# How many of a kernel's first loads may be in flight, and whether q goes ahead of w_in

## The chip, the cores and the metric

The kernel runs on one core of one Trainium2 chip. The metric is the time of one execution on the device in microseconds (us), taken as the median of several runs. Besides the plain runs one execution is recorded by the hardware profiler; all views below come from that one.

## The reference

Attention over a memory of 32 slots per head, followed by a feed-forward layer with SiLU. There are 8 batches, 8 heads, 576 positions and a head width of 64.

```python
a = softmax(phi, axis=2)                       # over the positions
k_m = einsum('bhsm,bhsd->bhmd', a, k)          # 32 memory keys per head
v_m = einsum('bhsm,bhsd->bhmd', a, v)          # 32 memory values per head
attn = softmax(q @ k_m.T / 8, axis=-1)         # over the 32 slots
x = (attn @ v_m) -> (4608, 512)
out = silu(x @ w_in) @ w_out                   # 512 -> 2048 -> 512
```

The weights are shared by all batches; `w_in` and `w_out` come in as raw 64-bit words and are turned into the format that TensorE uses by integer steps on ScalarE and VectorE.

## The kernel before

The work goes batch by batch (`for b in range(B)`, L875), and within a batch over 16 chunks of 128 columns of the hidden layer (`fc`). For a chunk, TensorE computes the hidden layer (`ffn1`, L627, line L642), ScalarE takes SiLU of it (`silu`, L662), VectorE splits it into a high and a low part (`split`, L651), and TensorE multiplies both with `w_out` (`ffn2`, L676, line L681). The attention of batch b+1 is laid between the chunks of batch b by a table of slots (L713 to L757).

Batch 0 has nothing before it. Its attention is written out by hand in the first block (L769 to L857), and in that block the instructions of VectorE and ScalarE stay in the order in which they are written (`in_order(DVE, ACT)`), as do those of TensorE throughout and those of SyncE's queue in batch 0. So an instruction that waits holds up all that stands behind it on its engine. The steps of the block that matter here, in order:

1. `load_phi(0)` (L217) and `load_kv(0)` (L226) issue the first loads. Batch 0's `kv` comes in four tiles and a rest (`kv0` to `kv3`, `kr`), all on ScalarE's DMA queue.
2. The loop over `LOADS` (L773) issues what follows, all on SyncE's queue: `i0` and `i1` are the two halves of the first piece of `w_in` (512 KB each), `Q0` and `Q1` the two halves of batch 0's `q` (576 KB each), `o0` and `o1` the two halves of the first piece of `w_out`, and each `L` a whole piece of weights.
3. `phi_max`, `phi_sub`, `phi_exp`: softmax numerators of phi, in two halves. `e_mm` (L319): memory keys and values, one `kv` tile after the other (L327), then the rest (L335), then the scaling to `kvn` (L349, L351).
4. `w_conv(I0, 0, "pc")` (L792): ScalarE's two steps (L167, L169) on the first half of the first piece of `w_in`, the one that `i0` loads.
5. `f_tr`, `f_vt` (L474), `f_scores(0)` (L485, needs `Q0`), `f_copy(0)` (L503 on ScalarE, L504 on VectorE), `f_turn(0)` (L517), `f_scores(1)` (L485, needs `Q1`), `f_max`, `f_sub` and so on, to the first chunk of the feed-forward layer.

`keep_warm` puts dummy matmuls of the identity between these steps on TensorE.

Loads that carry `few=True` wait, on SyncE, until an earlier load has landed: `load` (L86) keeps a list of all loads in the order of the program and ties the new one to the fifth before it.

Of the kernel before, what the change touches and what calls it, by code (L numbers as in the profile page):

```python
# [39 lines left out]
PHW = FULLC * HM + P  # L40
KVC = 2 * NR * KVW
RAWB = 3
LOADS = "i0 Q0 Q1 i1 o0 o1 L L L"
HOMES = {("o", 1): 8, ("i", 2): 12}
DEEP = 5


@with_exitstack
def attn_ffn_kernel(
# [34 lines left out]
    loads = []  # L84

    def load(dst, src, few=False, queue=None):  # L86
        i = (queue or nc.sync).dma_start(dst, src)
        if few:
            tc.add_manual_dep(
                i.ins,  # L90
                loads[-DEEP].ins.name,
                mybir.DependencyInfo(mybir.DependencyClass.Sync, mybir.DependencyReason.DATA),
                reason="few at a time",
            )
        loads.append(i)
# [25 lines left out]
    def w_load(w, part=None, few=False):  # L121


        kind, j = w
        if w not in raws:
            if w in HOMES:
                home = win[:, HOMES[w] : HOMES[w] + 4].rearrange("p k r f -> p (k r f)")
                raws[w] = home.bitcast(I64).rearrange("p (k f) -> p k f", k=2)
            else:
                raws[w] = sb.tile([P, 2, DMODEL], I64, tag="raw", name="raw", bufs=RAWB)  # L130
        if kind == "i":
            for k in range(2) if part is None else (part,):
                f = (2 * j + k) * P
                load(
                    raws[w][:, k].rearrange("p (r f) -> p r f", r=NR),
                    w_in[:, f : f + P].rearrange("(r p) f -> p r f", p=P),
                    few,
                )
        else:
            src = w_out[j * CW : (j + 1) * CW, :].rearrange("(r p) f -> p r f", p=P)  # L140
            load(w_part(raws[w], part), w_part(src, part), few)
# [75 lines left out]
    def load_phi(b):  # L217
        t = sb.tile([P, PHW], F32, tag="att", name=f"phi{b}")
        at[b]["e"] = t[:, : FULLC * HM].rearrange("p (g c f) -> p g c f", g=2, c=FULLC)
        at[b]["er"] = t[:, FULLC * HM :]  # L220
        at[b]["et"] = t
        w = FULLC * P
        for f in ((0, w), (2 * w, PHW), (w, 2 * w)) if b == 0 else ((0, PHW),):
            load(t[:, f[0] : f[1]], phi[b, :, f[0] : f[1]], queue=nc.scalar if f[0] == w else None)

    def load_kv(b):  # L226
        queue = nc.scalar if b == 0 else None
        ts = []
        for c in range(FULLC):
            t = sb.tile([P, 2, NR, KVW], F32, tag="kv", name=f"kv{b}_{c}", bufs=FULLC)  # L230
            load(t.rearrange("p g r f -> p (g r f)"), kv[b, :, c * KVC : (c + 1) * KVC], queue=queue)
            ts.append(t)
        t = sb.tile([P, NR, KVW], F32, tag="kr", name=f"kr{b}", bufs=1)
        load(t.rearrange("p r f -> p (r f)"), kv[b, :, FULLC * KVC :], queue=queue)
        at[b]["kv"], at[b]["kr"] = ts, t
# [533 lines left out]
    with in_order(DVE, ACT) as last:  # L769
        load_phi(0)  # L770
        nc.scalar.activation(tiny[:, :1], ident[:, :1], AF.Exp)
        load_kv(0)
        for c in LOADS.split():  # L773
            if c[0] == "Q":
# [181 lines left out]
```

## Time and profile before

| what | value |
|---|---|
| median of 3 runs | 703.94 us (703.69 to 704.26) |
| the profiled execution | 703.34 us |
| its span, first to last instruction | 701.6 us |
| granted TensorE clock, mean | 1.000 of full speed |
| busy share of TensorE, VectorE, ScalarE | 98%, 52%, 37% |
| chain that ended last: TensorE's share of it | 85% of the span |

The span is 1.7 us shorter than the profiled execution's time; the rest lies before the first and behind the last instruction. A busy TensorE includes the dummy matmuls. The share of busy time is an average over the whole program: the loads that the change touches are all issued in the first 15 us.

### The profile page before, as it was taken

How to read it: one execution, taken by the hardware profiler on the slowest of the kernel's cores; microseconds unless marked ns; L12 is line 12 of the kernel's file. 1: busy time of each engine (PE TensorE's matmuls, PEld its weight loads, DVE VectorE, ACT ScalarE, POOL GpSimd, SP SyncE). 2: the span in 40 equal slices, each digit the busy share in tenths (PEclk: the TensorE clock that was granted, in tenths of full speed). 3: DMA queues.
4: the chain of work that ended last, by engine and by line, in shares of the span. 5: the costliest groups of instructions: out<-in, count | busy, mean ns of one | idle time of the engine just before them, and what ended most of it. 6: DMA issues, size and time to landing. Idle time of an engine off the chain costs nothing.

```text
span 701.6 us, 11773 instructions
## 1 busy us (share of the span) xinstructions
PE 689.8 (98%) x4924; PEld 562.3 (80%) x4924; DVE 365.3 (52%) x665; ACT 259.1 (37%) x456; POOL 0.7 (0%) x6
## 2 busy tenths in 40 slices
PE   8999989999999999999999999999999999999997
PEld 3578768888888888888888888888888888888886
DVE  4898796425645256534636346542564525623322
ACT  3879674422414134421423314342241412431211
POOL 0000000000000000000000000000000000000000
PEclk9999999999999999999999999999999999999999
DMA  9995616122210221131110311112121000010002
GB/s 344 325 329 202 250 53 230 56 83 68 79 31 24 114 68 35 61 137 68 36 61 16 137 45 56 64 43 94 68 79 32 1 1 1 1 61 1 1 0 76
DMA packets 25445, 60.15 MB, mean 86 GB/s; under 512 B 2096, under 2 KB 10416, under 8 KB 25392
## 3 DMA queue, kind: packets, MB, share of 16 engines
q1 hardware_dynamic: 24448, 56.63, 22.8%
q10 hardware_dynamic: 944, 2.77, 1.0%
q8 instruction: 39, 0.64, 0.4%
q14 instruction: 14, 0.11, 0.0%
HBM read 49.95 MB, written 9.44 MB: 85 GB/s over the span
## 4 chain that ended last, share of the span: by engine, by line
PE 85%; DVE 1%; ACT 1%; issue 0%; ACTq 0%
PE acc L681 46%; PE h L642 26%; PE accleft L681 6%; PE bg L607 4%; PE h L327 2%; PE bg L372 1%; PE h L335 0%; PE h L357 0%; ACT L665 0%; DVE sc L420 0%; DVE wo_lo L177 0%; DVE raw L173 0%; PE h L372 0%; ACT wo_hi L175 0%; DVE sc L402 0%
## 5 line engine op out<-in xcount | busy, mean ns | idle before, releaser
L681 PE MATMUL acc<-wo_hi,gparts 128*128 128x512 f32 x1024 | 342.0, 395 | 1.0 <-DVE gparts L659 0.5
L681 PEld LDWEIGHTS acc<-wo_hi,gparts 128*128 128x128 f32 x1024 | 191.9, 188 | 54.2 <-issue 6.6
L642 PEld LDWEIGHTS h<-aparts,pparts 128*128 128x128 f32 x1524 | 213.9, 188 | 15.1 <-issue 2.5
L642 PE MATMUL h<-aparts,pparts 128*128 128x288 f32 x1524 | 223.1, 295 | 1.5 <-ACT gleft L667 1.2
L665 ACT ACTIVATE g<-h 128x512 f32<-128x512 f32 x127 | 76.1, 599 | 348.4 <-PE h L642 179.3
L681 PE MATMUL acc<-wo_lo,gparts 128*128 128x512 f32 x512 | 200.9, 392 | 0.6 <-DVE wo_lo L177 0.5
L657 DVE CAST gparts<-g 128x512 fp32r<-128x512 f32 x128 | 54.5, 426 | 261.0 <-ACT g L665 261.0
L681 PEld LDWEIGHTS acc<-wo_lo,gparts 128*128 128x128 f32 x512 | 96.1, 188 | 18.4 <-DVE wo_lo L177 1.9
L659 DVE TENSOR_TENSOR gparts<-g,gparts 128x512 fp32r<-128x512 f32 x128 | 88.2, 689 | 11.0 <-PE acc L681 0.5
L623 DVE TENSOR_TENSOR pparts<-bg,pparts 128x1024 fp32r<-128x1024 f32 (+1 forms) x36 | 39.7, 1102 | 5.4 <-ACT pparts L621 5.1
L681 PE MATMUL accleft<-wo_hi,gparts 128*128 128x512 f32 x128 | 40.6, 389 | 0.0
L621 ACT ACTIVATE pparts<-bg 128x1024 fp32r<-128x1024 f32 (+1 forms) x36 | 33.5, 931 | 14.3 <-PE bg L607 14.3
L607 PE MATMUL bg<-win,kvT 64*32 64x512 f32 (+1 forms) x576 | 35.8, 554 | 0.0
L681 PEld LDWEIGHTS accleft<-wo_hi,gparts 128*128 128x128 f32 x128 | 24.0, 188 | 4.9
L667 ACT ACTIVATE gleft<-h 128x64 f32<-128x64 f32 x127 | 27.8, 219 | 0.0
L688 ACT ACTIVATE o<-acc 128x512 f32<-128x512 f32 x32 | 19.2, 600 | 21.5 <-PE acc L681 10.6
L681 PE MATMUL accleft<-wo_lo,gparts 128*128 128x512 f32 x64 | 24.9, 389 | 0.0
L665 ACT ACT_TABLE_LOAD x14 | 18.0, 1283 | 14.1 <-issue 13.5
L657 DVE CAST gparts<-gleft 128x512 fp32r<-128x512 f32 x16 | 6.8, 427 | 20.7 <-PE accleft L681 12.2
L169 ACT ACTIVATE raw<-raw 128x1024 int32<-128x1024 uint32 (+1 forms) x16 | 16.9, 1053 | 0.0
L327 PEld LDWEIGHTS h<-kv,phi 128*32 128x32 f32 x384 | 10.2, 110 | 5.0 <-ACT gleft L667 5.0
L681 PEld LDWEIGHTS accleft<-wo_lo,gparts 128*128 128x128 f32 x64 | 12.0, 188 | 2.4
(139 smaller groups left out, 365.5 us busy)
## 6 DMA issues: line engine op xcount, KB each, us to landing
kv<-in_kv SPq DMA_DIRECT2D x28, 516.0 KB, 5.7
q<-in_q SPq DMA_DIRECT2D x16, 576.0 KB, 5.2
out<-o SPq DMA_DIRECT2D x32, 256.0 KB, 2.1
raw<-in_w_in SPq DMA_DIRECT2D x14, 512.0 KB, 6.4
raw<-in_w_out SPq DMA_DIRECT2D x6, 1024.0 KB, 5.3
phi<-in_phi SPq DMA_DIRECT2D x7, 576.0 KB, 3.7
kv<-in_kv ACTq DMA_DIRECT2D x4, 516.0 KB, 6.2
kr<-in_kv SPq DMA_DIRECT2D x7, 258.0 KB, 6.9
```

Of the source, the lines that this page charges most:

```text
L169: i = nc.scalar.activation(r, low, AF.Copy, scale=2.0**-29)
L327: nc.tensor.matmul(pt[p][M * r : M * (r + 1), :KVW], e[:, p, c, M * r : M * (r + 1)], kvt[c][:, p, r], start=c == 0, stop=False, skip_grou ...
L607: nc.tensor.matmul(bg[M * r : M * (r + 1), p, :w].rearrange("p (k f) -> p k f", f=P), kvT[D * p : D * (p + 1), 1, r], win[D * p : D * (p + ...
L621: nc.scalar.activation(hi[:, :, c], bg[:, :, :w], AF.Copy)
L623: nc.vector.tensor_tensor(lo[:, :, c], bg[:, :, :w], hi[:, :, c], op=ALU.subtract)
L642: nc.tensor.matmul(h[:, hf, :HALF], wt[:, p, fs], a[:, p, hf * HALF : (hf + 1) * HALF], start=n[hf] == 0, stop=n[hf] == 5, skip_group_chec ...
L657: nc.vector.tensor_copy(ghi, g32)
L659: nc.vector.tensor_tensor(glo, g32, ghi, op=ALU.subtract)
L665: nc.scalar.activation(g32.rearrange("p (h f) -> p h f", h=2), h[:, :, :w], AF.Silu)
L667: i = nc.scalar.activation(gleft[:, fc, o : o + LEFT].rearrange("p (h f) -> p h f", h=2), h[:, :, w:HALF], AF.Silu)
L681: nc.tensor.matmul(acc[key], gt[:, cs], wt[:, fc], start=fc == 0 and n == 0, stop=fc == NFC - 1 and n == 2)
L688: nc.scalar.activation(o, a, AF.Copy)
```

## The change

`LOADS` names `Q0` ahead of `i0`, so that each half of `q` stands in front of a half of `w_in`'s piece. And `load` ties a load to the third load before it rather than the fifth, as long as fewer than 11 loads are on the list.

```diff
-LOADS = "i0 Q0 Q1 i1 o0 o1 L L L"
+LOADS = "Q0 i0 Q1 i1 o0 o1 L L L"
 HOMES = {("o", 1): 8, ("i", 2): 12}
-DEEP = 5
+DEEP, FIRST_DEEP = 5, 3
...
             tc.add_manual_dep(
                 i.ins,
-                loads[-DEEP].ins.name,
+                loads[-(FIRST_DEEP if len(loads) < 11 else DEEP)].ins.name,
```

Eight loads stand on the list when the loop over `LOADS` begins: three of phi, then `kv0`, `kv1`, `kv2`, `kv3` and `kr`. So the new number holds for the loop's first three loads alone, which are now `Q0`, `i0` and `Q1`. What each load waits for:

| load | before | now |
|---|---|---|
| `i0` | `kv0` | `kv3` |
| `Q0` | `kv1` | `kv2` |
| `Q1` | `kv2` | `kr` |
| `i1` | `kv3` | `kv3` |
| `o0` | `kr` | `kr` |
| `o1` | `i0` | `Q0` |
| the two loads of the first `L` | `Q0`, `Q1` | `i0`, `Q1` |

On SyncE's queue, these are the first loads of the loop before. `raw<-in_w_in` is `i0`, later `i1`; `raw<-in_w_out` is `o0`; each `DMAHW` is a semaphore that a load raises when it lands, here those of `kv0` (3), `kv1` (4), `kv2` (5), `kv3` (7) and `kr` (1):

```order
L87 DMA phi_79<-in_phi 128x128
L87 DMA raw<-in_w_in 128x4x128 [waits DMAHW3_49]
L87 DMA q_0_96<-in_q 128x1152 [waits DMAHW4_49,DMAHW0_49]
L87 DMA q_1_98<-in_q 128x1152 [waits DMAHW5_49,DMAHW2_49]
L87 DMA raw<-in_w_in 128x4x128 [waits DMAHW7_49]
L87 DMA raw<-in_w_out 128x512 [waits DMAHW1_49]
```

And now, where `kv2` raises 5, `kv3` 6 and `kr` 7:

```order
L87 DMA phi_79<-in_phi 128x128
L87 DMA q_0_94<-in_q 128x1152 [waits DMAHW5_49,DMAHW0_49]
L87 DMA raw<-in_w_in 128x4x128 [waits DMAHW6_49,DMAHW1_49]
L87 DMA q_1_98<-in_q 128x1152 [waits DMAHW7_49,DMAHW2_49]
L87 DMA raw<-in_w_in 128x4x128 [waits DMAHW3_49]
L87 DMA raw<-in_w_out 128x512 [waits DMAHW4_49]
```

`i0` moved behind `Q0` and from `kv0`'s landing to that of `kv3`; `i1` and `o0` follow `Q1` without a wait of their own that is still open then. The waits on 0, 1 and 2 are for phi.

On ScalarE, in the same stretch, the order stays and the semaphores change hands:

```order
 L87 DMA kv_3_90<-in_kv 128x1032
-L87 DMA kr_92<-in_kv 128x516 [waits DMAHW1_49]
-L316 ACTIVATE phi_79<-phi_79 128x512 [waits DVE_49]
+L87 DMA kr_92<-in_kv 128x516
+L316 ACTIVATE phi_79<-phi_79 128x512 [waits DMAHW1_49,DVE_49]
 L317 ACTIVATE phi_79<-phi_79 64x128 [waits DMAHW2_49,DVE_49]
 L316 ACTIVATE phi_79<-phi_79 128x512 [waits DMAHW0_49,DVE_49]
 L317 ACTIVATE phi_79<-phi_79 64x128 [waits DVE_49]
 L349 ACTIVATE kvn<-first_152,rs 128x2x64 [waits DVE_49,PE_49]
-L167 ACTIVATE win<-raw 128x512 [waits DMAHW6_49]
+L167 ACTIVATE win<-raw 128x512 [waits DMAHW1_49]
```

The issue of `kr` no longer waits for a part of phi, whose semaphore it shared. `L167` still waits for `i0`, by another semaphore, and still stands ahead of `L474` and `L503` on ScalarE. TensorE's and VectorE's instructions keep their order.

## Rows read from the trace of the kernel before

**Rows 1.** The page, busy us (share of the span) x instructions of each engine

```profile
PE 689.8 (98%) x4924; PEld 562.3 (80%) x4924; DVE 365.3 (52%) x665; ACT 259.1 (37%) x456; POOL 0.7 (0%) x6
```

**Rows 2.** Stretches: us, busy us (x instructions) of PE, PEld, DVE, ACT, POOL, clock, DMA share, GB/s

```profile
17.00:31.00 14.00, 12.35 (x80) 7.47 (x80) 12.28 (x24) 11.44 (x22) 0.00 (x0) 1.00 1.06 366
31.00:60.00 29.00, 28.55 (x203) 22.19 (x202) 26.84 (x42) 23.75 (x33) 0.00 (x0) 1.00 0.81 289
```

**Rows 3.** Timeline of SyncE's DMA issues, 5 to 13 us: start us, us, what

```profile
5.82 0.38 SPq L87 DMA_DIRECT2D raw<-in_w_in  x1
7.62 0.34 SPq L87 DMA_DIRECT2D q<-in_q  x1
8.88 0.33 SPq L87 DMA_DIRECT2D q<-in_q  x1
10.27 0.38 SPq L87 DMA_DIRECT2D raw<-in_w_in  x1
11.39 1.22 SPq L87 DMA_DIRECT2D raw<-in_w_out  x2
```

**Rows 4.** DMA issues at 5.82 (i0) and 7.62 (Q0): KB, us to landing

```profile
raw<-in_w_in SPq DMA_DIRECT2D x1, 512.0 KB, 6.5
...
q<-in_q SPq DMA_DIRECT2D x1, 576.0 KB, 6.1
```

**Rows 5.** DMA queues, 5.8 to 9, then 9 to 11 us: packets, MB, share of 16 engines

```profile
q10 hardware_dynamic: 344, 1.23, 100.0%
...
q1 hardware_dynamic: 444, 0.47, 65.6%
q10 hardware_dynamic: 157, 0.31, 39.8%
```

**Rows 6.** DMA issues of w_in at 35.98, 61.84 and 62.26: KB, us to landing

```profile
raw<-in_w_in SPq DMA_DIRECT2D x1, 512.0 KB, 3.6
...
raw<-in_w_in SPq DMA_DIRECT2D x1, 512.0 KB, 3.9
...
raw<-in_w_in SPq DMA_DIRECT2D x1, 512.0 KB, 4.9
```

**Rows 7.** Timeline of ScalarE, 9.5 to 15 us: start us, us, what [idle before <-releaser]

```profile
9.57 0.63 ACT L316 ACTIVATE phi<-phi 128x512 f32<-128x512 f32 x1 [0.83 <-DVE phi L306]
...
12.64 0.37 ACT L349 ACTIVATE kvn<-first,rs 128x128 f32<-128x128 f32 x1 [2.11 <-DVE rs L345]
12.91 0.66 ACT L167 ACTIVATE win<-raw 128x512 f32<-128x512 f32 x1
13.47 0.67 ACT L169 ACTIVATE raw<-raw 128x512 int32<-128x512 uint32 x1
14.03 0.25 ACT L474 COPY kvT<-firstt 128x128 f32<-128x128 f32 x1
14.69 0.37 ACT L503 COPY sT<-firsts 128x256 f32<-128x256 f32 x1 [0.41 <-PE firsts L485]
```

**Rows 8.** Timeline of TensorE's matmuls, 9 to 16.5 us

```profile
9.18 0.87 PE L327 MATMUL first<-kv,phi 128*32 128x129 f32 x24
...
10.29 1.31 PE L327 MATMUL first<-kv,phi 128*32 128x129 f32 x40 [0.25 <-DMA kv<-in_kv]
11.53 0.45 PE L335 MATMUL first<-kr,phi 64*32 64x129 f32 x16
...
13.88 0.72 PE L485 MATMUL firsts<-q,kvT 64*32 64x288 f32 x16
14.54 0.60 PE L79 MATMUL spare<-ident 128*128 128x512 bf16 x2
15.12 0.66 PE L517 MATMUL firstu<-ident,sT 128*128 128x128 f32 x4
15.70 0.71 PE L485 MATMUL firsts<-q,kvT 64*32 64x288 f32 x16
```

**Rows 9.** Timeline of VectorE, 15 to 19 us

```profile
15.81 0.69 DVE L540 TENSOR_REDUCE fmx<-firstu 128x16 f32<-128x512 f32 x1
...
18.08 0.82 DVE L540 TENSOR_REDUCE fmx<-firstu 128x20 f32<-128x640 f32 x1 [0.85 <-PE firstu L519]
```

## The prediction, made before the changed kernel ran

> **What bounds the kernel now.** I read the page first. TensorE is busy for 98% of the span, VectorE and ScalarE for 52% and 37% [rows 1]. That average says little about the first 15 us, where the change sits, so I then read stretches. From 31 to 60 us TensorE is busy for 28.55 of 29.00 us, and from 17 to 31 us for 12.35 of 14.00, with VectorE at 12.28 beside it [rows 2]. The reader is to see that behind the opening there is no slack in which a late start could be made up: whatever the opening loses or gains arrives at the end of the program nearly whole. The question is thus how much later or earlier the opening's chain gets through.
>
> That chain I followed in the timelines of the engines. TensorE multiplies the first three `kv` tiles at 9.18, waits for `kv3`, goes on at 10.29 and takes the rest `kr` at 11.53 [rows 8]. ScalarE scales the result at 12.64, converts `i0`'s weights at 12.91 and 13.47, copies the transposed values at 14.03 and at 14.69 begins to copy the first scores [rows 7]. TensorE turns these at 15.12, computes the second scores at 15.70 [rows 8], and VectorE takes their maxima at 15.81 and 18.08 [rows 9], without a pause in the second case from the moment that TensorE delivered. Two facts about slack are to be seen here. Before the copy at 14.69 ScalarE stood idle for 0.41 us, waiting for TensorE's scores [rows 7]. So the conversion at 12.91 may start up to 12.91 + 0.41 = 13.32 without anything becoming late. From the copy on, each step starts at the end of the one before, so a later copy moves all.
>
> Then the loads. SyncE issued `i0` at 5.82, `Q0` at 7.62, `Q1` at 8.88, `i1` at 10.27 and `o0` at 11.39 [rows 3]. Each of these is the moment at which the load it waited for had landed: `kv0`, `kv1`, `kv2`, `kv3` and `kr`. `i0` took 6.5 us and landed at 12.3, `Q0` took 6.1 and landed at 13.7 [rows 4]: both just in time, 0.6 us ahead of ScalarE's 12.91 and 0.2 us ahead of TensorE's 13.88.
>
> **The change, part by part.**
>
> *`kr`'s issue.* It loses a wait on ScalarE's queue. From 5.8 to 9 us ScalarE's queue (q10) had the DMA engines to itself, at 100.0% [rows 5], so there was a backlog on it and an earlier issue of its last load brings nothing. Cost and gain: 0.
>
> *Fewer loads beside `kv`.* This can only help if `i0` and `Q0` took bandwidth from `kv` and `kr`. `i0` was issued at 5.82 [rows 3], but until 9 us SyncE's queue (q1) moved nothing: the only row of that stretch is q10's 1.23 MB [rows 5]. From 9 to 11 us q1 moved 0.47 MB and q10 its last 0.31 MB [rows 5]. I read this as first come, first served: an engine that had finished its share of `kv` went on with `i0`. Then `kv3` still lands at 10.27 and `kr` at 11.39. Bounds: no gain at one end. At the other, q10's 0.31 MB alone on the engines at the 0.78 MB in 2 us that both queues made takes 0.8 us and not some 2 us, so that `kr` lands at 10.4 and `kv3`, halfway, at 9.8. Even so, the second half of phi's exponentials ends at 9.57 + 0.63 = 10.20 [rows 7], and 32 of the 40 matmul records of the block at 10.29 need it. The block takes 11.53 - 10.29 = 1.24 us [rows 8], four fifths of it are 1.0, and the rest could start at 10.25 + 1.0 = 11.25: the gain is 0 to 0.3 us. I take 0, by the row up to 9 us.
>
> *`Q0` ahead.* It is now issued at `kv2`'s landing, 8.88 and not 7.62, with only q10's last 0.31 MB before it. A load of 512 KB that met a free queue took 3.6 to 3.9 us [rows 6]; 64 KB more at the same rate (0.78 MB in 2 us) is 0.2. So `Q0` lands at 12.7 to 13.0, ahead of the 13.88 at which TensorE wants it. Cost 0; the cover is 0.9 us, and the 6.1 us of before would overrun it by 1.1.
>
> *`i0` behind it.* This is the term that counts. It is now issued at `kv3`'s landing, 10.27, 4.45 us later than before. From below, 3.6 us from issue to landing; from above, 4.9 us, which is what the second of two such loads took when it was issued right behind the first [rows 6]. `Q0` runs 1.4 us ahead of `i0`, and its 0.59 MB take about 1.5 us at the rate above, so `i0` hardly queues; I take 3.9, the nearer row. `i0` then lands at 14.2, ScalarE starts on it at 14.3 (0.1 us from landing to start, as `kr`'s 11.39 to 11.53 shows), and that is 14.27 - 13.32 = 0.95 us too late. With 3.6 it is 0.65, with 4.9 it is 1.95.
>
> What is queued behind that wait: on ScalarE the copies at 14.03 and 14.69; on VectorE, in its order, the shift of the converted weights and then its own half of the first copy. TensorE waits for both halves with the turn at 15.12, and with it the second scores and VectorE's maxima. All are 0.95 us later. The conversions themselves (0.66 and 0.67 us, rows 7) are unchanged, only moved.
>
> *`Q1`, `i1`, `o0`.* They are issued together from 11.4 on, `Q1` 2.5 us later than before. `Q1` is wanted at 15.70 + 0.95 = 16.65, 5.2 us after its issue. Ahead of it lie the rest of `Q0` and `i0`, some 0.8 MB, then its own 0.59 MB: 1.4 MB at 0.39 MB per us is 3.6 us, and with some 1 us from the last byte to the landing (an estimate: `kr`'s last bytes moved before 11 us, and it landed at 11.39) it comes at about 16.0. Cost 0, with 0.6 us to spare; if it took the 6.1 us that `Q0` took before, it would come at 17.5 and make the whole delay 1.8. What waits behind them keeps its place, since all of it is late by about as much as its users are.
>
> **The sum**: 0 + 0 + 0 + 0.95 + 0 = 0.95 us. Against the profiled execution, 703.34 us (a span of 701.6 and 1.7 around it), that gives 704.3. The median of the runs is 703.94, 0.6 us above that execution, and carries the same shift: **704.9 us**, 0.13% more. About 0.2%, here 1.4 us, is what a measurement of this kernel can tell from no change; the forecast lies inside it.
>
> **The rivals.**
>
> *A: slower, `i0` queues behind `Q0`.* If some DMA engine is still busy with `kv`'s tail when `Q0` comes, `Q0` and then `i0` stack up on it. For it: q10 still moved data in the stretch from 9 to 11 us, after `Q0`'s new issue [rows 5], and the second load of a pair needed 4.9 us [rows 6]. Against it: the 1.4 us between the two issues. With 4.9 us the delay is 1.95 and the median 705.9. It decides from the point at which `i0` takes over 4.4 us from its issue: 10.27 + 4.4 + 0.1 - 13.32 is 1.4. Chance 0.18.
>
> *B: the queues share the engines.* If an engine goes back and forth between both queues, `kv`'s tail was slowed from 9 us on, and now is not. `e_mm` then ends 0.3 us earlier, and `i0` is issued at 9.8 and lands at 13.7; ScalarE's start at 13.8 is late by 13.8 - 13.32 = 0.5. The median is 704.4. For it: q10's share falls to 39.8% in the last 2 us [rows 5]. Against it: nothing of `i0` moved for 3 us after its issue. Chance 0.12. The Trainium skill has this as a rule ("DMA: Bandwidth & Descriptors", section "Queues, rings and completion order": each engine takes turns between the queue rows that have work, packet by packet). By that rule `i0` would have shared the engines with `kv` well before 9 us; the row up to 9 us does not agree with it.
>
> *C: `i0` is in time and `kv` gains.* This asks for a landing within 3.0 us of the issue, below every row in the group of loads that met a free queue. It would give 703.94 - 0.3 = 703.6. Chance 0.06. That the opening gains more than 1.4 us has no mechanism in the profile, as 10.20 bounds `e_mm`; I leave 0.04 for what I have not seen.
>
> **How the numbers follow.** The forecast has 0.64, A 0.18, B 0.12, C 0.06. The range goes from C's side, 703.8, to A's price, 705.9; outside lie most of C and the worst of A and of a late `Q1`, together under 0.2. Slower by over 0.2% is A and a little of the forecast's upper end: 0.20. Faster by over 0.2% is 0.04. Within it: 0.76.
>
> **What would show it.** Right: the issue of `Q0` near 8.9 and of `i0` near 10.3; the matmuls at 9.18, 10.29 and 11.53 where they were; a wait of ScalarE at L167 for the load, with L167 at 14.0 to 14.6; the copy L503 at 15.3 to 16.0 with no idle time before it; and every later step of the opening moved by as much. Wrong: `kr`'s matmuls before 11.3 (B), L167 after 14.8 or TensorE waiting for a half of `q` (A), or L167 still at 12.9 (C). A shift at L503 that has gone by 60 us would show that the stretches of rows 2 had slack after all.

## The result and the profile after

The changed kernel takes 706.91 us in the median of 7 runs (705.98 to 709.09), beside 704.13 for the kernel before on the same chip (7 runs): a ratio of 1.0044, with a 95% interval of 1.0032 to 1.0055. It is slower, and above the whole range that was forecast. The seven times fall into two groups: 705.98, 706.12, 706.52 and 706.91 with a mean granted clock of 0.998 to 0.999, and 708.61, 708.85 and 709.09 with 0.995. The execution recorded by the profiler is the last of these, with a span of 707.3 us: the views below show the longest of the seven.

The page hardly shows it: the busy times of the engines are those of [rows 1] to within 1 us, apart from TensorE, which is busy 2.5 us longer.

```profile
PE 692.3 (98%) x4924; PEld 563.3 (80%) x4924; DVE 365.2 (52%) x665; ACT 258.4 (37%) x456; POOL 0.7 (0%) x6
```

The timeline of SyncE's issues in the changed kernel, 8.5 to 14 us (start, length, what; to be read beside [rows 3]):

```profile
9.27 0.33 SPq L87 DMA_DIRECT2D q<-in_q  x1
10.54 0.38 SPq L87 DMA_DIRECT2D raw<-in_w_in  x1
11.20 0.34 SPq L87 DMA_DIRECT2D q<-in_q  x1
11.59 0.42 SPq L87 DMA_DIRECT2D raw<-in_w_in  x1
12.07 1.27 SPq L87 DMA_DIRECT2D raw<-in_w_out  x2
```

The DMA issues at 9.27 (`Q0`), 10.54 (`i0`), 11.20 (`Q1`) and 11.59 (`i1`), with KB and us to landing:

```profile
q<-in_q SPq DMA_DIRECT2D x1, 576.0 KB, 3.7
...
raw<-in_w_in SPq DMA_DIRECT2D x1, 512.0 KB, 6.5
...
q<-in_q SPq DMA_DIRECT2D x1, 576.0 KB, 7.3
...
raw<-in_w_in SPq DMA_DIRECT2D x1, 512.0 KB, 8.4
```

`Q0` lands at 12.99, as forecast, and its user starts at 14.11. Each load behind it takes longer than the one before: `i0` lands at 17.1, not 14.2, and `Q1` at 18.55, not 16.0. On ScalarE the conversion waits 3.87 us for `i0`; the copy of the scores stands right behind it, 3.69 us after its place in [rows 7]:

```profile
12.87 0.37 ACT L349 ACTIVATE kvn<-first,rs 128x128 f32<-128x128 f32 x1 [2.38 <-DVE rs L345]
17.11 0.66 ACT L167 ACTIVATE win<-raw 128x512 f32<-128x512 f32 x1 [3.87 <-DMA raw<-in_w_in]
...
18.38 0.38 ACT L503 COPY sT<-firsts 128x256 f32<-128x256 f32 x1
```

TensorE, in the same timeline form as [rows 8], is on time up to the first scores and then stands idle for 3.44 us:

```profile
10.52 1.31 PE L327 MATMUL first<-kv,phi 128*32 128x129 f32 x40 [0.52 <-DMA kv<-in_kv]
11.76 0.45 PE L335 MATMUL first<-kr,phi 64*32 64x129 f32 x16
...
14.11 0.72 PE L485 MATMUL firsts<-q,kvT 64*32 64x288 f32 x16
...
18.81 1.11 PE L517 MATMUL firstu<-ident,sT 128*128 128x128 f32 x4 [3.44 <-ACT sT L503]
19.85 1.21 PE L485 MATMUL firsts<-q,kvT 64*32 64x288 f32 x16
```

When it goes on, its matmuls take 1.11 and 1.21 us where they took 0.66 and 0.71. The stretches of the changed kernel say why (us, busy us and instructions of PE, PEld, DVE, ACT and POOL, granted clock, DMA share, GB/s):

```profile
10.00:16.00 6.00, 4.52 (x82) 2.09 (x81) 1.06 (x6) 0.83 (x3) 0.00 (x0) 1.00 0.93 282
16.00:18.00 2.00, 0.00 (x0) 0.00 (x0) 0.20 (x1) 0.89 (x2) 0.00 (x0) 1.00 1.05 344
18.00:20.00 2.00, 1.19 (x12) 0.86 (x20) 1.20 (x4) 0.93 (x5) 0.00 (x0) 0.50 0.98 372
...
22.00:24.00 2.00, 2.00 (x9) 1.40 (x8) 0.44 (x1) 1.51 (x3) 0.00 (x0) 0.50 1.09 355
24.00:25.00 1.00, 1.00 (x4) 0.36 (x3) 0.97 (x2) 0.00 (x0) 0.00 (x0) 0.59 1.06 408
25.00:31.00 6.00, 5.62 (x43) 2.52 (x41) 5.67 (x13) 5.48 (x8) 0.00 (x0) 1.00 0.95 312
```

The granted clock fell to 0.50, the lower of its two levels (1.2 of 2.4 GHz), at 18 us, while TensorE still stood idle, and stayed there until close to 25. VectorE's two maxima, the steps of [rows 9], are 4.15 and 5.48 us late, the second behind a further wait of 2.19 us for TensorE:

```profile
19.96 0.69 DVE L540 TENSOR_REDUCE fmx<-firstu 128x16 f32<-128x512 f32 x1 [0.80 <-PE firstu L517]
...
23.56 0.82 DVE L540 TENSOR_REDUCE fmx<-firstu 128x20 f32<-128x640 f32 x1 [2.19 <-PE firstu L519]
```

The span is 5.7 us longer than before: 3.69 from the wait, 1.8 that came in while the clock was low (5.48 less 3.69), and some 0.2 behind the opening. That nothing of it was made up there agrees with [rows 2].

The first line of the stretches, 10 to 16 us, holds the cause of the wait. The kernel before moved 392 GB/s in it:

```profile
10.00:16.00 6.00, 5.42 (x102) 2.69 (x101) 2.61 (x10) 2.79 (x9) 0.00 (x0) 1.00 1.06 392
```

With 282 GB/s the changed kernel is short of 110 GB/s for 6 us, 0.66 MB, or 1.7 us of transfers at the old rate, though four loads were issued by 11.6. The busy share of the DMA engines fell less than the rate, from 1.06 to 0.93: they were partly idle, and some of their packets took longer (both are shown below). The experiments ask why.

### The profile page after: what moved, and what is told of

It reads as the page before. It is cut to its first block, busy times and chain, and to the rows that moved or that the text cites. A ratio compares the mean times of both kernels' runs of the same rounds, so it can differ in the third digit from the quotient of the medians.

```text
span 707.3 us, 11775 instructions
## 1 busy us (share of the span) xinstructions
PE 692.3 (98%) x4924; PEld 563.3 (80%) x4924; DVE 365.2 (52%) x665; ACT 258.4 (37%) x456; POOL 0.7 (0%) x6
## 4 chain that ended last, share of the span: by engine, by line
PE 84%; DVE 1%; ACT 1%; issue 0%; ACTq 0%
PE acc L681 45%; PE h L642 26%; PE accleft L681 6%; PE bg L607 4%; PE h L327 2%; PE bg L372 1%; PE h L335 0%; PE h L357 0%; ACT L665 0%; DVE sc L420 0%; DVE wo_lo L177 0%; PE h L372 0%; DVE raw L173 0%; ACT wo_hi L175 0%; DVE sc L402 0%
## 5 line engine op out<-in xcount | busy, mean ns | idle before, releaser
L665 ACT ACT_TABLE_LOAD x14 | 18.0, 1283 | 14.4 <-issue 13.9
```

The costliest lines, as they stand in the source:

```text
L665: nc.scalar.activation(g32.rearrange("p (h f) -> p h f", h=2), h[:, :, :w], AF.Silu)
```

## The experiments

"Depth" below is the number of loads that may be in flight when one of the first three loads of the loop is issued (in `f1_two_behind`, the first six). A smaller depth also means a later issue, at the landing of a later load; most runs change both together. All edits are of the changed kernel unless the kernel before is named. The rate is that of 10 to 16 us in each profile.

| run | depth, order | median us (range, runs) | ratio to before (95%) | GB/s |
|---|---|---|---|---|
| the changed kernel | 3, `Q0 i0 Q1` | 706.91 (705.98 to 709.09, 7) | 1.0044 (1.0032 to 1.0055) | 282 |
| `e1_order` | 5, `Q0 i0 Q1` | 704.86 (704.64 to 706.64, 11) | 1.0013 (1.0004 to 1.0021) | 388 |
| `e5_before_late_conv` | 5, `i0 Q0 Q1` | 705.26 (704.73 to 706.36, 11) | 1.0018 (1.0009 to 1.0026) | 394 |
| `g2_depth4_i0_first` | 4, `i0 Q0 Q1` | 705.10 (704.63 to 706.45, 11) | 1.0018 (1.0009 to 1.0027) | 310 |
| `f2_depth4` | 4, `Q0 i0 Q1` | 705.24 (705.02 to 707.72, 7) | 1.0025 (1.0014 to 1.0036) | 309 |
| `e2_depth` | 3, `i0 Q0 Q1` | 708.50 (705.83 to 709.81, 6) | 1.0051 (1.0034 to 1.0068) | 270 |
| `e3_after_late_conv` | 3, `Q0 i0 Q1` | 707.03 (706.52 to 707.76, 5) | 1.0041 (1.0029 to 1.0053) | 296 |
| `f1_two_behind` | 3, then 2 | 708.50 (706.69 to 709.07, 4) | 1.0057 (1.0044 to 1.0070) | 221 |
| `f3_filler` | as 3, 512 KB in front | 706.57 (705.40 to 708.15, 5) | 1.0035 (1.0023 to 1.0047) | 365 |
| `g1_half_filler` | as 3, 256 KB in front | 707.52 (705.72 to 707.91, 5) | 1.0044 (1.0032 to 1.0057) | 339 |
| `e4_warm` | 3, 6 more dummies | 706.49 (706.08 to 710.09, 6) | 1.0041 (1.0026 to 1.0056) | 310 |
| `h1_warm14` | 3, 12 more dummies | 706.48 (706.25 to 707.74, 5) | 1.0038 (1.0025 to 1.0050) | 282 |

### Each half of the change alone

The order alone, in the kernel before:

```diff
-LOADS = "i0 Q0 Q1 i1 o0 o1 L L L"
+LOADS = "Q0 i0 Q1 i1 o0 o1 L L L"
```

> Only the order of LOADS is changed (Q0 ahead of i0), five loads stay in flight. Theory A (the whole cost is ScalarE's wait at L167 for i0): i0 is issued at kv1's landing near 7.6 and has Q0's 0.59 MB ahead of it, so it lands near 13.7 and L167 starts near 13.8; +0.3 to +0.8 us, about 704.6, clock 1.000. Rival B (the order is what costs, by Q0 and i0 in one queue): +2 us or more, with i0 landing after 15. Rival C (the later loads Q1, i1, o0 come late as well): here they do not, so it expects no change within 0.3 us.

Measured: 1.0013, a small loss of 0.7 us, and by a way that nobody had named; that theory A's +0.3 to +0.8 us holds it is luck. No load of SyncE's queue is late; the tail of `kv` is. TensorE waits for `kv3`, 1.0 us later than in [rows 8] (in every other profile it goes on between 10.29 and 10.69):

```profile
11.31 1.31 PE L327 MATMUL first<-kv,phi 128*32 128x129 f32 x40 [1.28 <-DMA kv<-in_kv]
```

From 9 to 11 us the queues of SyncE (q1) and ScalarE (q10) moved (packets, MB, share)

```profile
q1 hardware_dynamic: 90, 0.41, 51.1%
q10 hardware_dynamic: 164, 0.39, 49.9%
```

and in `e5_before_late_conv` below, which has `i0` in front and no less of `kv` left at 9 us,

```profile
q10 hardware_dynamic: 217, 0.51, 66.2%
q1 hardware_dynamic: 238, 0.24, 34.2%
```

The sums are alike, 0.80 and 0.75 MB, but with `Q0` in front `kv` got the smaller part and was not done by 11. What differs on q1 is the packet: `i0`'s are of 1 KB, `Q0`'s of 4.6 KB. The Trainium skill, "DMA: Bandwidth & Descriptors", section "Queues, rings and completion order", says that an engine alternates between the queues packet by packet. Larger packets on one queue would then take more of the engine from the other. This run agrees with that: from 10 to 10.5 us, while both queues moved, their packets were nearly equal in number and not in bytes.

```profile
q1 hardware_dynamic: 33, 0.15, 73.4%
q10 hardware_dynamic: 31, 0.06, 30.0%
```

That a packet of the trace is what the Trainium skill calls one is taken for granted here; no run shows it.

The depth alone, with `i0` in front:

```diff
-LOADS = "Q0 i0 Q1 i1 o0 o1 L L L"
+LOADS = "i0 Q0 Q1 i1 o0 o1 L L L"
```

> Only the depth is changed (three loads in flight for the first three loads of the loop), i0 stays ahead of Q0. i0 is then issued at kv2's landing near 9, Q0 at kv3's near 10.4. Theory A: i0 lands at 12.7 to 13.2, so L167 does not wait, but Q0 takes i0's place and lands at 14.3 to 17, so TensorE waits for it at L485 in place of 13.9; +0.5 to +3 us, 704.6 to 707. Rival B (the order is what costs): within 0.5 us of the kernel before. Rival C (the stream of loads is late as a whole): +2 us or more, also where neither i0 nor Q0 is waited for.

Measured: 1.0051, the whole loss and more than the 3 us that theory A allowed; the clock falls in its profile too. Now `i0`, first on the queue, takes 3.8 us and is converted at 13.29, and `Q0`, the second, takes 7.0. TensorE waits for it:

```profile
17.80 1.21 PE L485 MATMUL firsts<-q,kvT 64*32 64x288 f32 x16 [3.48 <-DMA q<-in_q]
```

Whichever load stands second is late. That is the work of the depth, in either order; the order alone costs 0.7 us, by the other way above.

### Is it the wait for i0 alone?

If ScalarE's wait for `i0` were the whole cost, moving its conversion away would give everything back. In this run and in its control, the kernel before with the same move, the conversion of `i0`'s half stands just ahead of `i1`'s:

```diff
-        w_conv(I0, 0, "pc")
...
-        w_conv(I0, 0, "s")
...
-        w_conv(I0, 0, "a")
...
+        w_conv(I0, 0, "pc")
...
+        w_conv(I0, 0, "sa")
```

> The changed kernel, with the conversion of i0's weights moved down in ScalarE's and VectorE's order, to just ahead of that of i1's weights. ScalarE no longer waits for i0 ahead of the copy of the first scores. Theory A: the copy L503 starts at 14.6 to 15.0 as in the kernel before, the clock stays at 1.000, and the time is that of the same move in the kernel before within 0.4 us, both at 704.5 to 705.5 (1.1 us more work on VectorE's chain). Rival C (Q1, i1 and o0 late as well): 1 us or more above the same move in the kernel before, with waits at L485, L500 or the second L167.

> The control for the run above: the kernel before with the same move of the conversion of i0's weights. All theories: L503 at 14.6 to 14.8, no wait for a load, clock 1.000, +0 to +1.3 us for the two conversion steps that now stand in VectorE's busy stretch from 19 us on, 704.1 to 705.4.

Measured: 707.03 and 705.26, so the depth still costs 1.8 us with the wait for `i0` gone. The copy L503 comes at 14.92, in time, and TensorE then waits for `Q1`, as the third load took 6.5 us:

```profile
15.34 0.66 PE L517 MATMUL firstu<-ident,sT 128*128 128x128 f32 x4
17.83 0.72 PE L485 MATMUL firsts<-q,kvT 64*32 64x288 f32 x16 [1.83 <-DMA q<-in_q]
```

Theory A falls, and rival C holds. `i0` is the first of several late loads.

### Four loads in flight

```diff
-DEEP, FIRST_DEEP = 5, 3
+DEEP, FIRST_DEEP = 5, 4
```

> The changed kernel with a depth of four in place of three: Q0 is issued at kv1's landing near 7.8, i0 at kv2's near 9.1, Q1 at kv3's near 10.4. Theory D (the dry queue): Q0 is at hand when the queue of kv drains, so the rate from 10 to 13 us stays near 390 GB/s, i0 lands at 13.9 to 14.6, L167 starts then, and the time is 704.5 to 705.5. Theory B (bunched loads): still three loads issued within 2 us behind i0, so i0 lands after 16 and the time is 706 or more.

Measured: 705.24, in the range of theory D, but not for its reason: the rate from 10 to 13 us is 290 to 330 GB/s and not near 390. `i0`, issued at 9.4, takes 5.5 us, lands between the two forecasts, and ScalarE waits:

```profile
14.98 0.66 ACT L167 ACTIVATE win<-raw 128x512 f32<-128x512 f32 x1 [1.56 <-DMA raw<-in_w_in]
```

The same depth in the order of the kernel before, as an edit of that kernel:

```diff
-DEEP = 5
+DEEP, FIRST_DEEP = 5, 4
...
-                loads[-DEEP].ins.name,
+                loads[-(FIRST_DEEP if len(loads) < 11 else DEEP)].ins.name,
```

> The kernel before with four loads in flight in place of five among the first eleven, in its own order (i0, Q0, Q1). If what counts is how long a load is issued ahead of its first data: i0 is issued near 7.6 and Q0 near 8.9 to 9.2 us, Q0 takes its 5 to 6 us and lands at 14.3 to 15, TensorE waits 0.4 to 1.1 us for it at L485, and the median is 704.5 to 705.3. If only the step to three loads starves the engines, nothing is late, and the median is within 0.3 us of the kernel before.

Measured: 705.10, with `Q0` issued at 9.16 and taking 5.9 us, as the first theory had it:

```profile
15.22 0.72 PE L485 MATMUL firsts<-q,kvT 64*32 64x288 f32 x16 [1.15 <-DMA q<-in_q]
```

So it is not only the step to three that starves the engines. In both orders the rate goes from 388 to 394 GB/s at a depth of five to 309 and 310 at four and 270 to 310 at three: the loss of rate begins with the first load taken away.

### Does the second load suffer from those behind it?

SyncE issues `Q1`, `i1` and `o0` within 1.6 us after `i0`; perhaps they take engines from it. This run lets only two loads be in flight from `i0` on, so that `Q1` waits for `Q0`, `i1` for `i0`:

```diff
-loads[-(FIRST_DEEP if len(loads) < 11 else DEEP)].ins.name,
+loads[-(FIRST_DEEP if len(loads) < 10 else 2 if len(loads) < 14 else DEEP)].ins.name,
```

> The changed kernel, but from Q1 on a load waits for the second one before it (Q1 for Q0, i1 for i0, o0 for Q1, o1 for i1), so that nothing is queued behind i0 until Q0 has landed. Theory B (the loads issued together behind i0 take its bandwidth): i0 lands 3.6 to 4.9 us after its issue, at 14.2 to 15.5, and L167 starts then. Theory D (the queue ran dry, and the loads after a dry queue are slow whatever is behind them): i0 still needs 5.5 us or more. Either way Q1 is issued at 13 and lands at 17 or later, so the time is no measure here: 707 to 710.

Measured: 708.50. `i0`, issued at 10.69, still takes 6.3 us, and until `Q1`'s issue at 14.64 nothing stood behind it:

```profile
raw<-in_w_in SPq DMA_DIRECT2D x1, 512.0 KB, 6.3
```

Theory B falls as the whole cause. Nor can `i0` have been waiting for engines at their full rate: from 12 to 13 and from 13 to 14 us they moved 269 and 327 GB/s.

### Does a DMA engine that runs dry start slowly?

In the changed kernel ScalarE's queue runs out between 9.5 and 11 us, just when `Q0`, issued at 9.27, brings its first packets. The queues of the changed kernel from 10 to 10.5 us:

```profile
q1 hardware_dynamic: 13, 0.06, 99.1%
q10 hardware_dynamic: 42, 0.07, 38.0%
```

and q1 from 11.5 to 12 us:

```profile
q1 hardware_dynamic: 43, 0.20, 98.2%
```

A share of 16 engines over 0.5 us is 8 us of packet time: the 13 packets took 0.61 us each, the 43 later ones, of the same 4.6 KB, 0.18. In the kernel before every packet of `Q0` took 0.18 to 0.21. The theory was that engines which ran dry start slowly, and that work in the queue over this moment would cure it. Two runs put a later piece of `w_in` in front of `Q0`, issued at `kv0`'s landing (5.9 us), and left the ties of `Q0`, `i0` and `Q1` as they are. The first adds 512 KB:

```diff
-LOADS = "Q0 i0 Q1 i1 o0 o1 L L L"
+LOADS = "x Q0 i0 Q1 i1 o0 o1 L L y"
...
-loads[-(FIRST_DEEP if len(loads) < 11 else DEEP)].ins.name,
+loads[-(4 if 8 < len(loads) < 12 else DEEP)].ins.name,
...
+            elif c[0] == "x":
+                w_load(("i", 2), 0, True)
+            elif c[0] == "y":
+                w_load(next(to_load), 1, True)
```

> The changed kernel with one more load in front: half of a later piece of w_in (512 KB, wanted only after 33 us) is issued at kv0's landing near 5.9, and Q0, i0 and Q1 wait for kv2, kv3 and kr as in the changed kernel. Theory D (the dry queue): the filler bridges the gap, the rate from 10 to 13 us is near 390 GB/s, and although 0.52 MB more stand ahead of them, i0 lands at 13.8 to 15 and Q1 at 15.3 to 16.5, both earlier than in the changed kernel (17.05 and 18.5); 704.6 to 706, below the changed kernel. Theory B (bunched loads) or a plain shortage of bandwidth: i0 lands at 17 or later and the time is at or above the changed kernel's.

The second adds 256 KB; `half_load` is a part of `w_load` with half the rows:

```diff
+            elif c[0] == "x":
+                half_load(0, slice(0, 2))
+            elif c[0] == "y":
+                next(to_load)
+                half_load(0, slice(2, 4))
+                w_load(("i", 2), 1, True)
```

> The changed kernel with 256 KB of a later piece of w_in (half of a half) loaded in front of Q0, from the landing of kv0 on, and Q0, i0 and Q1 tied to the landings of kv2, kv3 and kr as in the changed kernel; the other half of that piece is loaded last. If the engines that ran dry near 10 us are the cost: the rate from 10 to 13 us is above the changed kernel's 206, 355 and 226 GB/s, i0 lands at 14.4 to 15.2 although 0.26 MB more stand ahead of it, L503 comes at 15.9 to 16.7, and the median is 705.3 to 706.2. If bytes ahead of i0 are what counts, i0 lands later than the 17.09 of the changed kernel and the median is 707 or more.

Measured: 706.57 and 707.52, neither clearly below the changed kernel's 706.91. What the theory said of 10 us came true, and what it said of the time did not. With 256 KB in front:

```profile
10.00:12.00 2.00, 1.52 (x60) 1.22 (x56) 0.00 (x0) 0.55 (x2) 0.00 (x0) 1.00 1.06 407
12.00:13.00 1.00, 1.00 (x19) 0.21 (x3) 0.62 (x5) 0.07 (x1) 0.00 (x0) 1.00 0.72 224
```

The rate from 10 to 12 us is up to 407 GB/s, and `Q0`'s packets are quick. But from 12 to 13, where `i0`'s first data are due, it falls to 224: the hole has moved to the next load. `i0`, issued at 10.59, takes 5.8 us and lands at 16.4. The median is where the expectation put it for the rival, bytes ahead of `i0`; the landing, not later than 17.09, is not. With 512 KB in front `i0` takes 4.8 and lands at 15.4, and TensorE's wait is half of what the changed kernel's profile has:

```profile
17.09 0.66 PE L517 MATMUL firstu<-ident,sT 128*128 128x128 f32 x4 [1.73 <-ACT sT L503]
```

That is not shown to be the filler's doing, though: in `e4_warm` and `h1_warm14` below, with the same loads and no filler, `i0` lands at 15.4 and 15.7. What the two runs show is that bytes ahead of `i0` are not what makes it late, and that the hole at 10 us is not the only one.

In each profile with a depth of four or three there is such a hole, with idle engines and single packets of 0.5 to 1.9 us, near the first data of a load that was issued some 1 to 2 us earlier; `i0` in the kernel before had been issued 3.4 us before its first data, near 9.2. The first loads that had a lead of 3 us or more (`i0` and `Q0` at a depth of five, and the two fillers) met no hole: none of their packets took over 0.35 us. But not every short lead brought one (`Q0` behind the fillers was quick), so what it is about a short lead that makes the hole is left open. In five of these profiles an instruction fetch (queue q8) also holds one engine for 0.9 to 1.4 us between 13 and 15.5 us, and may add to the lateness there; in the changed kernel it comes at 17.9, behind `i0`'s landing, so it is not the cause.

### What does the clock add?

Dummy matmuls ahead of the first turn keep TensorE busy in the wait, 6 more in one run and 12 more in another:

```diff
-        keep_warm(spare, 2)
+        keep_warm(spare, 8)
```

> The changed kernel with six more dummy matmuls (some 1.4 us) behind the first scores, where TensorE waited for 3.4 us. If the fall of the granted clock is a cost of its own: the clock stays at 1.00 throughout, the copy L503 is as late as in the changed kernel, and the runs that had a clock of 0.995 (708.6 to 709.1) are gone, so the median falls to 705.5 to 706.5. If the clock costs nothing beside the wait: the same times as the changed kernel, 706.0 to 709.1.

```diff
-        keep_warm(spare, 2)
+        keep_warm(spare, 14)
```

> The changed kernel with 12 more dummy matmuls in front of the first turn of scores, so that TensorE is busy through the whole wait for i0; by the length of a dummy they end near 18.1 us. The turn (L517) cannot start before that, 3.0 us later than its 15.12 in the kernel before, whichever load is late. If the fall of the granted clock is a cost of its own, on top of the wait: every run shows a clock of 0.998 or more, the median is 704.1 + 3.0 to 3.6 = 707.1 to 707.7, and no run is at 708.6 or above, where three of seven runs of the changed kernel lie. If the runs near 709 come from something else than the clock, they are still there.

Measured: 706.49 with 6 more, five runs at 706.08 to 707.10 with a clock of 0.999 to 1.000, and one at 710.09 with 0.995, so six do not seem to keep the clock in every run. In the profile with 6 more, at the full clock, ScalarE waits for `i0` less long than in the changed kernel's:

```profile
15.44 0.66 ACT L167 ACTIVATE win<-raw 128x512 f32<-128x512 f32 x1 [2.10 <-DMA raw<-in_w_in]
```

With 12 more, no run above 707.74, and 0.999 or more in all five. Its profile (the dummies end at 17.69, earlier than expected) has TensorE go on without idle time at the full clock, 2.57 us behind [rows 8], and is 2.9 us longer in its span:

```profile
15.70 0.67 ACT L167 ACTIVATE win<-raw 128x512 f32<-128x512 f32 x1 [2.57 <-DMA raw<-in_w_in]
```

```profile
14.66 3.20 PE L79 MATMUL spare<-ident 128*128 128x512 bf16 x14
17.69 0.60 PE L517 MATMUL firstu<-ident,sT 128*128 128x128 f32 x4
```

With 12 more the times near 709 are gone, as they should be if they came from the clock; that is likely rather than certain, as three such times dealt at random among the twelve runs of the two kernels would all miss these five about once in six. The loss of some 2 to 3 us stays, of which the dummies themselves make some 0.3 (the turn follows L503 by 0.43 us in [rows 7] and [rows 8], and here L503 comes at 16.99). The profiles agree: the clock fell during or within 1 us behind an idle time of TensorE of 2.67 (`g1_half_filler`), 2.68 (`f1_two_behind`), 3.44 (the changed kernel) and 3.48 us (`e2_depth`), and stayed at 1.00 after 1.13 (`f2_depth4`), 1.73 (`f3_filler`) and 1.83 (`e3_after_late_conv`).

## Why the prediction was wrong

- *What bounds the opening, and that nothing is made up behind it*: right. Span and L503 moved together where L503 was what came late and the clock held: by 1.6 and 1.56 us in `f2_depth4`, by 2.0 and 1.97 in `f3_filler`, by 1.2 and 1.32 in `g2_depth4_i0_first`; only in `e4_warm`, with 2.7 and 2.02, less closely.
- *`kr`'s issue, and fewer loads beside `kv`*: right, 0. TensorE's matmuls of 10.29 and 11.53 in [rows 8] came 0.23 us later, not earlier. Rivals B and C, which needed a gain there, have nothing for them. B's premise, that the queues share the engines, has: `e1_order` agrees with it, and not with the prediction's "first come, first served".
- *`Q0` ahead*: the landing, 12.99, is at the end of the 12.7 to 13.0 that were forecast, partly by luck: the issue was 0.39 us late, and the load took 3.7 us and not 3.8 to 4.1. With the same loads it took 4.4 and 4.7 in the profiles with the dummies, and landed at 13.7, still in time.
- *`i0` behind it*: **this step failed.** The place was right (ScalarE's wait at L167, then L503 with no idle time), the size was not: "`i0` hardly queues; I take 3.9, the nearer row". It took 6.5 us in the profile of the changed kernel, 5.7 in `e3_after_late_conv`, and 4.8 and 5.2 in those with the dummies; the upper bound, 4.9, was no bound, and the 0.95 us at L503 became 3.69. The arithmetic of the queue was not what failed: in the kernel before, `i0`, `Q0`, `Q1` and `i1` land 1.4 to 1.5 us apart (12.27, 13.70, 15.17, 16.64), and at that pace `i0` would have landed at 14.4, behind `Q0`'s 12.99. What failed was that the engines would keep that pace with three loads in flight: they moved 282 GB/s and not 392. The rows of the group were loads met one or two at a time; none showed a second or third load right after the engines had emptied.
- *`Q1`, `i1`, `o0`*: failed by the same assumption. "1.4 MB at 0.39 MB per us" took a rate that [rows 5] show only with five loads in flight; measured was 0.28. `Q1` came at 18.55, not 16.0; in `e3_after_late_conv`, where it took 6.5 us and not 7.3, it alone cost 1.8 us. The price of a late `Q1` had been worked out, 1.8, and given no chance of its own.
- *The clock*: not considered. It adds 1.8 us in the profile of the changed kernel, and the middle one of the three runs at 0.995, 708.85, lies 2.5 us above the middle of the other four, 706.3.
- *Rival A*: its price, 705.9, is just under the fastest run, 705.98, and its place is right. Its reason is not: `i0` did not stack up behind a busy engine. The engines had gaps, and with 0.52 MB more in front of it (`f3_filler`) `i0` came no later.
- *The chances*: 0.64, 0.18, 0.12 and 0.06 make 1.00, and the 0.04 that was left for the unseen stands beside them: 1.04 in all.

The sum with what was measured: 1.9 to 2.8 us over the 704.13 of before in 4 runs of 7, for which waits for late loads are enough; in the other three 4.5 to 5.0, in the one of them that was profiled a longer wait with the fall of the clock behind it.

## What to carry to other kernels

In this kernel a limit on loads in flight set the rate that the engines reached, and not only the order in which data came: price a smaller limit by a stretch of the trace with as few loads in flight, and where there is none, leave the range open above. A row of a load that met empty engines shows that load's own time (3.6 to 3.9 us here); what the second and third behind it take is another number (4.8 to 7.8). Where the wait it makes leaves TensorE idle, look up in the trace what the granted clock does after such an idle time.

## What the runs showed of the hardware

- A load lands when the slowest of its 16 engines is done. The trace has one landing event per engine: `i0`'s came between 11.34 and 12.27 us in the kernel before, and between 14.21 and 17.09 in the changed one, 14 of them by 15.17. The Trainium skill has this in "DMA: Bandwidth & Descriptors", section "Why a DMA increments its semaphore by 16 and not by 1": each engine that takes part counts up by one when its own share has landed. The trace agrees, with 16 events for each load.
- The last two of `i0`'s 16 engines made half of its lateness in the changed kernel: without them ScalarE could have gone on 1.9 us earlier. No engine lagged so in `e4_warm` and `h1_warm14`, where the 16 events lie within 1.3 us. That such laggards are what parts the runs at 0.995 from the others is a guess, as only one execution of the changed kernel was profiled.
- 1 KB and 4.6 KB packets on one queue did not weigh alike on the other queue: in `e1_order`, `Q0` ahead of `i0` made TensorE's start on `kv3` 1.0 us later, with as much moved by both queues from 9 to 11 us (0.80 against 0.78 MB). That the packet's size is the reason is argued from one run, and not shown.
- In the changed kernel, packets of 4.6 KB took 0.18 us on the steady queue and 0.61 us on average, up to 1.06, on the queue that had just begun; in `g1_half_filler` they took 0.18 from the start.
